# Writing out the first column group of a QKV projection piece by piece, in another order and with part of the work on GpSimd

## The chip, the cores and the metric

The kernel runs on one core of one Trainium2 chip. The metric is the device time of one launch in microseconds (us). Three runs of the kernel before gave 1294.83, 1295.52 and 1296.1; the median is 1295.52 us.

## The reference

2048 tokens with 576 channels, all float32. The input is normalised once, `xn = layernorm(x)`, and two branches of `xn` are added to `x`:

```
def _A_ref(x, wqkv, wo):              # 32 heads of 18, window 8, dilation 2
    qkv = x @ wqkv                    # 576 -> 1728
    ...                               # softmax over 8 dilated earlier positions
    return o @ wo

def _B_ref(x, w1, w2, w3, w4):
    h = gelu(layernorm(x) @ w1)       # 576 -> 576, its quarters shifted by +1, -1, +2, -2 tokens
    x1 = x + shifted(h) @ w2
    return x1 + gelu(layernorm(x1) @ w3) @ w4     # 576 -> 4608 -> 576

return x + _A_ref(xn, wqkv, wo) + _B_ref(xn, w1, w2, w3, w4)
```

The change touches only the beginning of `xn @ wqkv`: the first 288 of its 1728 output columns for the first 512 tokens.

## The kernel before, in words

**Split products.** Every float32 operand of a matrix product is split into a high part (the value rounded to TensorE's fp32r type) and a low part (value minus high part). A product is the sum of high*high, high*low and low*high. The inner dimension of 576 is cut into four slices of 128 and a tail of 64. In the tail, partitions 0 to 63 hold the high part of the tokens and 64 to 127 their low part, against weight rows that are loaded twice. So there are ten slots of weights (0 to 3 high, 4 the tail's high, 5 to 8 low, 9 the tail's low) and nine of tokens, and a tile of 128 tokens by 288 columns takes the 14 matmuls in `PAIRS`: four high*high, four high*low, four low*high and two of the tail.

**Stages.** The kernel goes through the QKV projection (with the transposed second layer norm), the mixer's first product with its shifts, its second product, then the MLP in 36 chunks of the hidden dimension with the attention woven in on VectorE, and the output projection. Instructions of each engine stay in the order in which the code issues them (`manual_schedule`); what an instruction must wait for is a semaphore of the engine or DMA that makes its data or frees its buffer.

**The stage of the change.** Tokens come in tiles of 128 (`load_x`, three buffers `xin`). For tiles 0 to 3, `stats` (L83 to L90) takes mean and variance on VectorE (two `bn_stats`, one `bn_aggr`, one add) and the inverse square root on GpSimd (L89, a `pow` on 128x1); `norm_x` (L96) writes the normalised tile to `Y`. `prep_x` calls `transposes` (L98 to L117): four TensorE transposes (L104) and one of the tail (L107) into PSUM, ScalarE copies the high parts to `xt` (L109 main, L112 tail), VectorE subtracts to get the low parts (L113 main, L116 tail). The weights come in column groups (`COLS`: 288, 288, 288, 432, 432 columns): `load_cg` loads one, `split_cg` has ScalarE write the high part (L167) and VectorE the low part (L168). `q_cg` (L276) makes the 14 matmuls of one tile and one group, ordered high*high, high*low, low*high, tail; ScalarE copies the result to `stg` (L279) and SP stores it (`spill`, L264). A `mid` function can be put before the last three matmuls of a `q_cg`; tiles 2 and 3 are transposed there.

**Order before.** VectorE: stats of tiles 0 and 1, norms 0 and 1, low parts of weight slices 0 to 3, token low parts of tile 0, weight slice 4, stats 2, token low parts 1, norm 2, stats 3, token low parts 2, norm 3, token low parts 3, then the low parts of column group 1. TensorE: 24 warming transposes, the transposes of tiles 0 and 1, then the 14 matmuls of tile after tile with the transposes of tiles 2 and 3 inside. After tile 3, the other column groups follow (`for cg in range(1, 5)`) with tokens that are all there.

Of the kernel before, what the change touches and what calls it, by code (L numbers as in the profile page):

```python
# [8 lines left out]
F32 = mybir.dt.float32  # L9
F32R = mybir.dt.float32r  # L10
AF = mybir.ActivationFunctionType
ALU = mybir.AluOpType
# [28 lines left out]
def dram_ap(t, offset, dims):  # L41
    return bass.AP(tensor=t.tensor, offset=t.offset + offset, ap=[list(d) for d in dims])
# [3 lines left out]
def fused_block(ctx, tc, x, wqkv, wo, w1, w2, w3, w4, out):  # L46
    nc = tc.nc
    pe, act, dve, pool, sp = nc.tensor, nc.scalar, nc.vector, nc.gpsimd, nc.sync
# [6 lines left out]
    psa = ctx.enter_context(tc.tile_pool(name="psa", bufs=2, space=PSUM))  # L55
    psb = ctx.enter_context(tc.tile_pool(name="psb", bufs=3, space=PSUM))
    dram = ctx.enter_context(tc.tile_pool(name="dram", bufs=1, space=DRAM))

    Y = base.tile([128, NT, D], F32, name="Y")
    ident = base.tile([128, 128], F32, name="ident")  # L60
# [13 lines left out]
    def tail_half(t):  # L74
        if t % 2 == 0:
            ztail[t // 2] = qpool.tile([128, 128], F32, name="ztail", bufs=2)
        return ztail[t // 2][:, t % 2 * 64:t % 2 * 64 + 64]

    def pair_tail(src, xts, t):
        return (src, [(xts, (t % 4 - 1) * 128), (xts, (t % 4) * 128)]) if t % 2 else None  # L80

    def stats(src, kind, t):
        st = BN[:, bncnt[0] % 4]  # L83
        bncnt[0] += 1
        for h in range(2):
            dve.bn_stats(out=st[:, h, :], in_=src[:, h * HF:(h + 1) * HF])
        dve.bn_aggr(out=MV[kind][:, t, :], in_=st)
        dve.tensor_scalar(RS[kind][:, t, 0:1], MV[kind][:, t, 1:2], 1e-5, None, op0=ALU.add)
        pool.tensor_tensor(RS[kind][:, t, 1:2], RS[kind][:, t, 0:1], mhalf, op=ALU.pow)  # L89
        if kind == 2:  # L90
            neg = MV[kind][:, t, 0:1]
            dve.tensor_scalar(neg, neg, -1.0, None, op0=ALU.mult)
            pool.tensor_tensor(RS[kind][:, t, 0:1], neg, RS[kind][:, t, 1:2], op=ALU.mult)

    def norm(dst, src, kind, t):
        dve.tensor_scalar(dst, src, MV[kind][:, t, 0:1], RS[kind][:, t, 1:2],  # L96
                          op0=ALU.subtract, op1=ALU.mult)

    def transposes(src, tail, xt, col):
        ps = psb.tile([128, 2, 512], F32, name="ps", tag="b")  # L100
        p0 = ps[:, 0, :].rearrange("p (k c) -> p k c", k=4)
        p1 = ps[:, 1, :128]
        for k in range(4):
            pe.transpose(p0[:, k, :], src[:, k * 128:(k + 1) * 128], ident)  # L104
        rows = tail[0].shape[1] if tail else 0
        if tail:
            pe.transpose(p1[:rows], tail[0], ident)  # L107
        c = slice(col, col + 128)
        act.copy(xt[:, 0:4, c], p0)  # L109
        for i in range(rows // 64):  # L110
            xtt, ct = tail[1][i]
            act.copy(xtt[0:64, 4, ct:ct + 128], p1[64 * i:64 * i + 64])  # L112
        dve.tensor_tensor(xt[:, 5:9, c], p0, xt[:, 0:4, c].bitcast(F32), op=ALU.subtract)  # L113
        for i in range(rows // 64):
            xtt, ct = tail[1][i]
            dve.tensor_tensor(xtt[64:128, 4, ct:ct + 128], p1[64 * i:64 * i + 64],  # L116
                              xtt[0:64, 4, ct:ct + 128].bitcast(F32), op=ALU.subtract)  # L117
# [48 lines left out]
    def split_w(dst_hi, dst_lo, raw):  # L166
        act.copy(dst_hi, raw)  # L167
        dve.tensor_tensor(dst_lo, raw, dst_hi.bitcast(F32), op=ALU.subtract)  # L168

    def dup_tail(dst, w, col, n):  # L170
        ncols = w.shape[1]
        for a in range(2):
            sp.dma_start(dst[64 * a:64 * a + 64, :],
                         dram_ap(w, 512 * ncols + col, [[ncols, 64], [1, n]]))

    def main_rows(dst, w, col, n, k0=0, k1=4):
        sp.dma_start(dst, w[k0 * 128:k1 * 128, col:col + n].rearrange("(k p) c -> p k c", p=128))
# [19 lines left out]
    qpool = qp.__enter__()  # L197
    WQ = qpool.tile([128, 10, 3 * D], F32R, name="WQ")
    xtile = {}
    xring = {}  # L200
    CG = 432
    COLS = [(0, 288), (288, 288), (576, 288), (864, 432), (1296, 432)]

    def load_x(t):
        xtile[t] = qpool.tile([128, D], F32, name="xin", bufs=3)
        sp.dma_start(xtile[t], xf[t * 128:(t + 1) * 128, :])

    def norm_x(t):
        norm(Y[:, t, :], xtile[t], 0, t)
        if t >= 4:  # L210
            dve.tensor_copy(tail_half(t), Y[:, t, 512:])

    def ring_block(key):
        if key not in xring:
            xring[key] = ring.tile([128, 9, 512], F32R, name="xt", tag="xt")
        return xring[key]

    def prep_x(t):
        xt = ring_block(("q", t // 4))
        if t < 4:  # L220
            tail = (Y[:, t, 512:], [(xt, t * 128)])
        else:
            tail = pair_tail(ztail[t // 2], xt, t)
        transposes(Y[:, t, :], tail, xt, (t % 4) * 128)

    qraw = {}

    def load_cg(cg, pieces):
        c, n = COLS[cg]
        r = qraw[cg] = qpool.tile([128, 5, n], F32, name="raw", bufs=2)  # L230
        if pieces:
            main_rows(r[:, 0:2, :], wqkv, c, n, 0, 2)
            main_rows(r[:, 2:4, :], wqkv, c, n, 2, 4)
        else:
            main_rows(r[:, 0:4, :], wqkv, c, n)
        dup_tail(r[:, 4, :], wqkv, c, n)

    def split_cg(cg, k0, k1):
        c, n = COLS[cg]
        split_w(WQ[:, k0:k1, c:c + n], WQ[:, 5 + k0:5 + k1, c:c + n], qraw[cg][:, k0:k1, :])  # L240
# [17 lines left out]
    def lhs(t):  # L258
        xt = xring[("q", t // 4)]
        c = (t % 4) * 128  # L260
        return lambda s: xt[:, s, c:c + 128]

    def spill(stg, t, c0, n):
        sp.dma_start(qkvd[c0 // GC:(c0 + n) // GC, HALO + t * 128:HALO + (t + 1) * 128, :]  # L264
                     .rearrange("s p d -> p s d"),
                     stg.rearrange("p (s d) -> p s d", d=GC))

    def q_cg(t, cg, mid=None):
        ps = psb.tile([128, 2, 512], F32, name="ps", tag="b")
        xs = lhs(t)  # L270
        c, n = COLS[cg]
        pairs = sorted(PAIRS, key=lambda p: (p[0] >= 4, p[1] >= 4))
        for i, (a, b) in enumerate(pairs):
            if mid and i == 11:
                mid()
            pe.matmul(ps[:, 0, :n], xs(a), WQ[:, b, c:c + n],  # L276
                      start=i == 0, stop=i == len(pairs) - 1)
        stg = qpool.tile([128, 2 * CG], F32, name="stg", bufs=4)
        act.copy(stg[:, :n], ps[:, 0, :n])  # L279
        spill(stg[:, :n], t, c, n)  # L280
# [10 lines left out]
    def x_stage(t):  # L291
        norm_x(t)
        prep_x(t)
        stats(Y[:, t, :], 1, t)
# [23 lines left out]
    warm = psa.tile([128, 512], F32, name="p1", tag="a")  # L318
    for i in range(24):
        pe.transpose(warm[:, :128], ident, ident)  # L320
    stats(xtile[0], 0, 0)
    stats(xtile[1], 0, 1)
    norm_x(0)
    norm_x(1)
    split_cg(0, 0, 1)
    split_cg(0, 1, 2)
    split_cg(0, 2, 3)
    split_cg(0, 3, 4)
    prep_x(0)
    split_cg(0, 4, 5)  # L330
    stats(xtile[2], 0, 2)
    prep_x(1)
    q_cg(0, 0)
    norm_x(2)
    load_x(4)
    load_cg(2, False)
    stats(xtile[3], 0, 3)
    q_cg(1, 0, lambda: prep_x(2))
    norm_x(3)
    q_cg(2, 0, lambda: prep_x(3))  # L340
    split_cg(1, 0, 3)
    split_cg(1, 3, 5)
    load_cg(3, False)
    q_cg(3, 0)
    sp.dma_start(dram_ap(qkvd[8:9, 0:1, :], 0, [[(HALO + S) * GC, 16], [1, HALO * GC]]), zpad)
    for cg in range(1, 5):
        for t in range(4):
# [123 lines left out]
    for b in range(NB):  # L471
        for i, m in enumerate((0, 1, 2, 4, 3) if b < 3 else (4, 0, 1, 2, 3)):
# [12 lines left out]
            k = {(0, 4): 0, (1, 1): 1, (1, 4): 2, (2, 1): 3, (2, 4): 4}.get((b, i))  # L485
# [46 lines left out]
    for t in range(NT):  # L532
        ps = psb.tile([128, 2, 512], F32, name="ps", tag="b")

        def xs(a, t=t):
            if a == 4:
                return T4[:, 2 + t * 128:2 + (t + 1) * 128]
            p, g = divmod(a, 5)
            c = 2 + t * 128 - SHIFT[g]
            return H[p][g][:, c:c + 128]  # L540
# [12 lines left out]
        if t in (9, 10, 13, 14):  # L553
            k = {9: 4, 10: 6, 13: 8, 14: 10}[t]
# [280 lines left out]
    for t in range(NT):  # L835
        b, s = divmod(t, 4)
# [7 lines left out]
        if t < NT - 1:  # L844
            ps = psb.tile([128, 2, 512], F32, name="ps", tag="b")
# [3 lines left out]
        else:  # L849
            for h in range(2):  # L850
                ph = psa.tile([128, 512], F32, name="p1", tag="a")
                for i, (a, w) in enumerate(PAIRS):
                    pe.matmul(ph[:, :HF], oT(a), Wo[:, w, h * HF:(h + 1) * HF],  # L853
                              start=i == 0, stop=i == len(PAIRS) - 1)
# [30 lines left out]
```

## Time and profile before

| what | value |
|---|---|
| median of three runs | 1295.52 us (1294.83 to 1296.1) |
| the profiled execution's own time | 1294.73 us |
| its span, first to last instruction | 1292.9 us |
| TensorE (PE) busy | 1285.0 us, 99% |
| weight load (PEld) busy | 1184.8 us, 92% |
| VectorE (DVE) busy | 935.6 us, 72% |
| ScalarE (ACT) busy | 362.0 us, 28% |
| GpSimd (POOL) busy | 38.1 us, 3% |
| granted TensorE clock | 0.9 or more of full speed in all slices (1.000 as the core's mean) |

A line of the timeline reads: start in us from the span's start, duration in us, engine, line of the kernel, operation, output and inputs by the program's names, shapes, how many such instructions were merged into the row, and in brackets how long the engine was idle before and what released it. PE is the matmul and PEld the loading of its stationary operand, which runs beside the matmul before. Matmuls are pipelined, so their durations overlap; the starts of weight loads show the pace. In the view by windows, "(x)" is the number of instructions that lie in the stretch.

### The profile page before, as it was taken

The page shows a single profiled execution, that of the slowest core. Times are in us where ns is not written, and L with a number is a line of the kernel's source. Part 1 is how long each engine was busy: PE and PEld are TensorE (multiplying, and loading weights), DVE is VectorE, ACT ScalarE, POOL GpSimd, SP SyncE. Part 2 cuts the span into 40 slices and gives each one's busy share as a digit, 9 for nine tenths or more (in the row PEclk, how much of TensorE's full clock was granted, in tenths as well). Part 3 has the DMA queues.
Part 4 walks back from the last instruction along what each step waited for, and adds up shares of the span by engine and source line. Part 5 has one row for each costly group of instructions (what it writes and reads, how often), then busy time and mean ns, then how long its engine had stood idle before and what let it go on. Part 6 is the DMA issues. An engine that isn't in the chain of part 4 may idle for free.

```text
span 1292.9 us, 18505 instructions
## 1 busy us (share of the span) xinstructions
PE 1285.0 (99%) x7678; PEld 1184.8 (92%) x7678; DVE 935.6 (72%) x1336; ACT 362.0 (28%) x601; POOL 38.1 (3%) x108
## 2 busy tenths in 40 slices
PE   8999999999999999999999999999999999999998
PEld 8999998899899999989999999999998999999998
DVE  6455534689576778888878888878888878855741
ACT  3332126524412232232222132232232231213310
POOL 2011100021000000000000000000000000000000
PEclk9999999999999999999999999999999999999999
DMA  7646884346702030221221221221232111156842
GB/s 204 154 122 137 172 174 143 92 108 155 229 29 73 29 101 20 82 75 46 82 73 48 82 72 42 89 73 29 75 99 71 31 49 44 58 120 158 208 145 83
DMA packets 157828, 125.20 MB, mean 97 GB/s; under 512 B 72608, under 2 KB 129824, under 8 KB 157744
## 3 DMA queue, kind: packets, MB, share of 16 engines
q1 hardware_dynamic: 157744, 124.02, 34.9%
q8 instruction: 60, 0.98, 0.3%
q14 instruction: 24, 0.20, 0.0%
HBM read 83.56 MB, written 39.39 MB: 95 GB/s over the span
## 4 chain that ended last, share of the span: by engine, by line
PE 94%; DMA 2%; DVE 2%; ACT 1%; SPq 0%; issue 0%; ACTq 0%
PE ps L696 35%; PE p L676 34%; PE ps L182 17%; PE ps L431 4%; PE ps L276 3%; DMA xd<-st 1%; PE ps L446 1%; PE ps L104 1%; DMA xt<-xd 0%; DMA raw<-in_A_wqkv_dram 0%; DMA x1n<-xd 0%; DVE st L129 0%; SPq L137 0%; PE p L853 0%; ACT rz L523 0%
## 5 line engine op out<-in xcount | busy, mean ns | idle before, releaser
L696 PE MATMUL ps<-W,hi 128*128 128x288 f32 x2304 | 398.7, 294 | 0.5 <-DVE Y L699 0.4
L696 PEld LDWEIGHTS ps<-W,hi 128*128 128x128 f32 x2304 | 339.5, 188 | 7.2 <-DVE Y L699 1.0
L680 ACT ACTIVATE hi<-p 128x512 fp32r<-128x512 f32 x144 | 86.2, 598 | 578.4 <-PE p L676 578.4
L696 PE MATMUL ps<-W,lo 128*128 128x288 f32 x1152 | 245.3, 294 | 0.0
L676 PE MATMUL p<-x1n,W 128*128 128x512 f32 x1008 | 234.6, 389 | 0.0
L676 PE MATMUL p<-xt,W 128*128 128x512 f32 x1008 | 234.4, 389 | 0.0
L676 PEld LDWEIGHTS p<-xt,W 128*128 128x128 f32 x1008 | 187.3, 188 | 36.9
L676 PEld LDWEIGHTS p<-x1n,W 128*128 128x128 f32 x1008 | 187.3, 188 | 36.8
L699 DVE TENSOR_TENSOR Y<-ps,Y 128x576 f32<-128x576 f32 x288 | 212.0, 748 | 11.0 <-PE ps L696 10.7
L682 DVE TENSOR_TENSOR lo<-g,hi 128x512 fp32r<-128x512 f32 x144 | 99.5, 691 | 159.5 <-ACT g L681 159.4
L696 PEld LDWEIGHTS ps<-W,lo 128*128 128x128 f32 x1152 | 185.3, 187 | 0.0
L182 PE MATMUL ps<-WQ,xt 128*128 128x432 f32 x672 | 134.4, 359 | 0.0
L182 PEld LDWEIGHTS ps<-WQ,xt 128*128 128x128 f32 x672 | 125.5, 188 | 5.4
L628 DVE TENSOR_TENSOR prod<-q,k 128x1152 f32<-128x1152 f32 x64 | 86.4, 1349 | 0.0
L631 DVE TENSOR_REDUCE L<-prod 128x64 f32<-128x1152 f32 x64 | 86.1, 1346 | 0.0
L681 ACT ACTIVATE g<-p 128x512 f32<-128x512 f32 x144 | 85.3, 592 | 0.0
L612 DVE TENSOR_TENSOR o<-o,prod 128x1152 f32<-128x1152 f32 x56 | 75.5, 1349 | 0.0
L608 DVE TENSOR_TENSOR prod<-v,L 128x1152 f32<-128x1152 f32 x56 | 75.5, 1348 | 0.0
L167 ACT CAST W<-rawf 128x640 fp32r<-128x640 f32 x72 | 50.3, 700 | 70.5 <-PE ps L696 69.2
L168 DVE TENSOR_TENSOR W<-rawf,W 128x640 fp32r<-128x640 f32 x72 | 56.2, 783 | 0.0
L182 PE MATMUL ps<-W,h 128*128 128x288 f32 x384 | 53.5, 295 | 0.0
L182 PEld LDWEIGHTS ps<-W,h 128*128 128x128 f32 x384 | 51.9, 188 | 0.1
(108 smaller groups left out, 888.7 us busy)
## 6 DMA issues: line engine op xcount, KB each, us to landing
xd<-st SPq DMA_DIRECT2D x48, 320.0 KB, 6.0
qkvd<-stg SPq DMA_DIRECT2D x24, 432.0 KB, 3.6
rawf<-in_B_w_dram SPq DMA_DIRECT2D x36, 288.0 KB, 3.2
rawf<-in_B_w_dram SPq DMA_DIRECT2D x36, 256.0 KB, 3.0
xt<-xd SPq DMA_DIRECT2D x8, 768.0 KB, 5.1
xin<-in_A_x_dram SPq DMA_DIRECT2D x16, 288.0 KB, 3.8
q<-qkvd SPq DMA_DIRECT2D x8, 576.0 KB, 4.0
k<-qkvd SPq DMA_DIRECT2D x8, 576.0 KB, 5.0
```

The costliest lines, as they stand in the source:

```text
L168: dve.tensor_tensor(dst_lo, raw, dst_hi.bitcast(F32), op=ALU.subtract)
L182: pe.matmul(ps[:, h, :n], xs(a), ws(b, h), start=i == 0, stop=i == len(PAIRS) - 1)
L608: dve.tensor_tensor(dst, vv, Lf[:, :, w:w + 1].to_broadcast([128, TPP * GH, HD]), op=ALU.mult)
L612: dve.tensor_tensor(o, o, dst, op=ALU.add)
L628: dve.tensor_tensor(prod.rearrange("p (j h) d -> p j (h d)", h=GH), q, k[:, r0:r0 + TPP, :], op=ALU.mult)
L631: dve.tensor_reduce(Lf[:, :, w], prod, axis=AX.X, op=ALU.add)
L676: pe.matmul(ps, W3[f][:, w, :], x1n[b][:, a, :], start=n == 0, stop=n == len(PAIRS) - 1)
L680: act.activation(by_token(hi), in_order(ps), AF.Gelu_apprx_tanh)
L681: act.activation(by_token(g32), in_order(ps), AF.Gelu_apprx_tanh)
L682: dve.tensor_tensor(lo, g32, hi.bitcast(F32), op=ALU.subtract)
L696: pe.matmul(ps[:, k, :HF], h[:, col], w[:, p, k * HF:(k + 1) * HF], start=n == 0, stop=n == len(seq) - 1)
L699: dve.tensor_tensor(yv, ps[:, :, :HF], yv, op=ALU.add)
```

## The change

Only the part for tiles 0 to 3 and column group 0 is written anew. `stats` is cut in two functions (`bn_halves` and `moments`) with the same instructions. In place of `split_cg(0, ...)`, `prep_x(0..3)` and `q_cg(0..3, 0)`, single pieces are issued:

- the low parts of weight slices 0, 1, 2 and 4 are GpSimd's (`w_lo(pool, k)`), that of slice 3 stays VectorE's;
- the products of tiles 0 and 1 accumulate in two PSUM buffers of the pool `psa` at the same time, in parts (`HH` high*high, `HL` high*low, `LH` low*high, `TL` tail), and their tails come after the transposes of tile 2;
- VectorE's norm 0 goes ahead of the last steps of stats 1, and the token low parts of tile 0 ahead of everything after norm 1;
- ScalarE's order is weight slices 0 and 1, tokens of tile 0, weight slices 2 and 3, the tail of tile 0, weight slice 4, tiles 1 and 2, and then the two results of tiles 0 and 1;
- on SP, the load of tile 4 and that of column group 2 are issued ahead of the first three stores, not after the first of them.

The number of instructions is the same on ScalarE; on VectorE it is less by four and on GpSimd more by four.

```
+    def w_lo(eng, k):
+        eng.tensor_tensor(WQ[:, 5 + k, c0:c0 + n0], qraw[0][:, k, :],
+                          WQ[:, k, c0:c0 + n0].bitcast(F32), op=ALU.subtract)
...
+    def x_lo(t):
+        p0, p1, c = main_tail(t)
+        dve.tensor_tensor(xt0[:, 5:9, c], p0, xt0[:, 0:4, c].bitcast(F32), op=ALU.subtract)
+        dve.tensor_tensor(xt0[64:128, 4, c], p1, xt0[0:64, 4, c].bitcast(F32), op=ALU.subtract)
...
     stats(xtile[0], 0, 0)
-    stats(xtile[1], 0, 1)
+    st1 = bn_halves(xtile[1])
     norm_x(0)
+    x_turned(0)
+    w_hi(0)
+    w_hi(1)
+    moments(st1, 0, 1)
+    w_lo(pool, 0)
+    w_lo(pool, 1)
+    x_hi(0)
+    w_hi(2)
+    w_hi(3)
+    x_tail_hi(0)
+    w_hi(4)
     norm_x(1)
-    split_cg(0, 0, 1)
-    split_cg(0, 1, 2)
-    split_cg(0, 2, 3)
-    split_cg(0, 3, 4)
-    prep_x(0)
-    split_cg(0, 4, 5)
+    q_part(0, HH, True)
+    x_turned(1)
+    x_lo(0)
+    q_part(0, LH)
+    w_lo(pool, 2)
+    x_hi(1)
+    x_tail_hi(1)
     stats(xtile[2], 0, 2)
-    prep_x(1)
-    q_cg(0, 0)
+    w_lo(dve, 3)
+    w_lo(pool, 4)
+    q_part(1, HH, True)
+    q_part(0, HL)
+    x_lo(1)
+    q_part(1, LH)
+    q_part(1, HL)
     norm_x(2)
     load_x(4)
     load_cg(2, False)
+    x_turned(2)
     stats(xtile[3], 0, 3)
-    q_cg(1, 0, lambda: prep_x(2))
+    x_hi(2)
+    x_tail_hi(2)
+    q_part(0, TL)
+    q_out(0)
+    q_part(1, TL)
+    q_out(1)
+    q_part(2, HH, True)
+    q_part(2, HL)
+    x_lo(2)
+    q_part(2, LH)
     norm_x(3)
-    q_cg(2, 0, lambda: prep_x(3))
+    x_turned(3)
+    q_part(2, TL)
+    x_hi(3)
+    x_tail_hi(3)
+    q_out(2)
+    x_lo(3)
     split_cg(1, 0, 3)
     split_cg(1, 3, 5)
     load_cg(3, False)
-    q_cg(3, 0)
+    for pairs in (HH, HL, LH, TL):
+        q_part(3, pairs, pairs is HH)
+    q_out(3)
```

`x_turned`, `x_hi` and `x_tail_hi` hold the instructions of `transposes`, `w_hi` and `w_lo` those of `split_w`, `q_part` and `q_out` those of `q_cg`.

More of the change, by code (lines that the diff above doesn't have):

```diff
@@ L82, in stats, with bn_halves @@
     def stats(src, kind, t):
+        moments(bn_halves(src), kind, t)
+    def bn_halves(src):
         st = BN[:, bncnt[0] % 4]
@@ L86, in stats, with moments @@
             dve.bn_stats(out=st[:, h, :], in_=src[:, h * HF:(h + 1) * HF])
+        return st
+    def moments(st, kind, t):
         dve.bn_aggr(out=MV[kind][:, t, :], in_=st)
@@ L320, in fused_block, with w_hi, main_tail @@
         pe.transpose(warm[:, :128], ident, ident)
+    c0, n0 = COLS[0]
+    xt0 = ring_block(("q", 0))
+    tps, qps = {}, {}
+    def w_hi(k):
+        act.copy(WQ[:, k, c0:c0 + n0], qraw[0][:, k, :])
+    def w_lo(eng, k):
+        eng.tensor_tensor(WQ[:, 5 + k, c0:c0 + n0], qraw[0][:, k, :],
+                          WQ[:, k, c0:c0 + n0].bitcast(F32), op=ALU.subtract)
+    def main_tail(t):
+        c = slice(t * 128, t * 128 + 128)
+        return (tps[t][:, 0, :].rearrange("p (k c) -> p k c", k=4), tps[t][:64, 1, :128], c)
@@ new lines, in x_turned, with x_hi, x_tail_hi @@
+    def x_turned(t):
+        tps[t] = psb.tile([128, 2, 512], F32, name="ps", tag="b")
+        p0, p1, c = main_tail(t)
+        for k in range(4):
+            pe.transpose(p0[:, k, :], Y[:, t, k * 128:(k + 1) * 128], ident)
+        pe.transpose(p1, Y[:, t, 512:], ident)
+    def x_hi(t):
+        p0, p1, c = main_tail(t)
+        act.copy(xt0[:, 0:4, c], p0)
+    def x_tail_hi(t):
+        p0, p1, c = main_tail(t)
+        act.copy(xt0[0:64, 4, c], p1)
+    def x_lo(t):
+        p0, p1, c = main_tail(t)
+        dve.tensor_tensor(xt0[:, 5:9, c], p0, xt0[:, 0:4, c].bitcast(F32), op=ALU.subtract)
+        dve.tensor_tensor(xt0[64:128, 4, c], p1, xt0[0:64, 4, c].bitcast(F32), op=ALU.subtract)
@@ new lines, in fused_block, with q_part, q_out @@
+    HH = [(k, k) for k in range(4)]
+    HL = [(k, k + 5) for k in range(4)]
+    LH = [(k + 5, k) for k in range(4)]
+    TL = [(4, 4), (4, 9)]
+    def q_part(t, pairs, first=False):
+        if first:
+            qps[t] = psa.tile([128, 512], F32, name="p1", tag="a")
+        xs = lhs(t)
+        for i, (a, b) in enumerate(pairs):
+            pe.matmul(qps[t][:, :n0], xs(a), WQ[:, b, c0:c0 + n0], start=first and i == 0,
+                      stop=pairs is TL and i == len(TL) - 1)
+    def q_out(t):
+        stg = qpool.tile([128, 2 * CG], F32, name="stg", bufs=4)
+        act.copy(stg[:, :n0], qps[t][:, :n0])
+        spill(stg[:, :n0], t, c0, n0)
```

## The prediction

> **What bounds the kernel now.** First the page's busy shares, then a table by windows, then the timeline of the first 21 us engine by engine (the stage of the change), and the chain of waits between its rows.
>
> ```profile
> PE 1285.0 (99%) x7678; PEld 1184.8 (92%) x7678; DVE 935.6 (72%) x1336; ACT 362.0 (28%) x601; POOL 38.1 (3%) x108
> ```
> ```profile
> 0.00:20.45 20.45, 16.26 (x101) 14.32 (x102) 13.14 (x34) 8.38 (x19) 4.72 (x22) 1.00 0.69 202
> ```
>
> TensorE is busy 1285.0 us, and the profiled execution took 1294.73 us with a span of 1292.9 us, so 7.9 us of the span are idle. In the window up to 20.45 us 16.26 us are busy: 4.19 us of the idle time lie there, in what this change rewrites. After it the kernel is bound by matmuls, so a microsecond won or lost here reaches the end nearly whole; but 4.19 us, 0.3%, is all that there is to win, and the part of it before the first tile has arrived is out of reach.
>
> Inside the stage VectorE sets the pace. Its timeline:
>
> ```profile
> 6.05 0.21 DVE L87 BATCH_NORM_AGGREGATE mv<-bn 128x2 f32<-128x12 f32 x1
> 6.30 0.15 DVE L88 TENSOR_SCALAR rs<-mv 128x1 f32<-128x1 f32 x1
> 6.37 0.57 DVE L96 TENSOR_SCALAR Y<-xin,mv,rs 128x576 f32<-128x576 f32 x1
> 7.38 0.58 DVE L96 TENSOR_SCALAR Y<-xin,mv,rs 128x576 f32<-128x576 f32 x1 [0.44 <-POOL rs L89]
> 7.88 1.56 DVE L168 TENSOR_TENSOR WQ<-raw,WQ 128x288 fp32r<-128x288 f32 x4
> 9.35 0.69 DVE L113 TENSOR_TENSOR xt<-ps,xt 128x512 fp32r<-128x512 f32 x1
> 10.07 0.28 DVE L116 TENSOR_TENSOR xt<-ps,xt 64x128 fp32r<-64x128 f32 x1
> 10.39 0.46 DVE L168 TENSOR_TENSOR WQ<-raw,WQ 128x288 fp32r<-128x288 f32 x1
> 10.77 0.81 DVE L86 BATCH_NORM_STATS2 bn<-xin 128x6 f32<-128x288 f32 x2
> ...
> 11.94 0.69 DVE L113 TENSOR_TENSOR xt<-ps,xt 128x512 fp32r<-128x512 f32 x1
> 12.66 0.28 DVE L116 TENSOR_TENSOR xt<-ps,xt 64x128 fp32r<-64x128 f32 x1
> 12.98 0.58 DVE L96 TENSOR_SCALAR Y<-xin,mv,rs 128x576 f32<-128x576 f32 x1
> ...
> 15.25 0.69 DVE L113 TENSOR_TENSOR xt<-ps,xt 128x512 fp32r<-128x512 f32 x1 [0.54 <-ACT xt L112]
> 15.97 0.28 DVE L116 TENSOR_TENSOR xt<-ps,xt 64x128 fp32r<-64x128 f32 x1
> 16.29 0.58 DVE L96 TENSOR_SCALAR Y<-xin,mv,rs 128x576 f32<-128x576 f32 x1
> ```
>
> Up to norm 2 at 12.98 it hardly pauses. From there on it is a chain through three engines: norm, transposes, ScalarE's copies, VectorE's token low parts, next norm, 3.31 us from norm 2 (12.98) to norm 3 (16.29). The weight loads and ScalarE show the other links:
>
> ```profile
> 13.67 0.42 PEld L104 LDWEIGHTS ps<-ident,Y 128*128 128x128 f32 x4 [0.56 <-issue]
> ...
> 16.98 0.42 PEld L104 LDWEIGHTS ps<-ident,Y 128*128 128x128 f32 x4 [0.38 <-issue]
> ...
> 18.43 2.82 PEld L276 LDWEIGHTS ps<-WQ,xt 128*128 128x128 f32 x21 [0.51 <-ACT xt L109]
> ```
> ```profile
> 7.09 0.76 ACT L167 CAST WQ<-raw 128x288 fp32r<-128x288 f32 x2 [0.46 <-DMA raw<-in_A_wqkv_dram]
> 7.80 0.59 ACT L109 CAST xt<-ps 128x512 fp32r<-128x512 f32 x1
> 8.28 0.26 ACT L112 CAST xt<-ps 64x128 fp32r<-64x128 f32 x1
> ...
> 14.47 0.58 ACT L109 CAST xt<-ps 128x512 fp32r<-128x512 f32 x1 [2.74 <-PE ps L107]
> 14.96 0.26 ACT L112 CAST xt<-ps 64x128 fp32r<-64x128 f32 x1
> 15.11 0.40 ACT L279 COPY stg<-ps 128x288 f32<-128x288 f32 x1
> ```
>
> From norm start to transposes 0.69 us (12.98 to 13.67), from these to the main copy 0.80 (14.47), to the token low parts 0.78 more (15.25), to the next norm 1.04 (16.29). Tile 3's products start at 18.43, and 2.82 us for 21 weight loads is 0.134 us each: from there the engine runs without pause. So the change is worth what it moves the transposes of tile 3, at 16.98 before.
>
> **The change part by part.** I follow the new order with these durations.
>
> *Norm 0 earlier.* It needs the bn_stats ahead of it (over by 6.05) and GpSimd's pow (over at 6.01, row below): 6.05 in place of 6.37, 0.32 us won. By tile 0's own rows (6.37 to 7.80, 1.43) ScalarE's main copy starts at 7.48. Statistics 1 end after it: aggregate at 6.55 (a norm holds VectorE 0.50, 7.38 to 7.88), add 0.25 later, pow from 7.03 (0.23 after the add) to 7.58, norm 1 from 7.61 to 8.19, 0.23 later than before. That is harmless: the transposes of tile 1 now stand behind four matmuls which wait for weight slice 3, until about 8.9.
>
> *ScalarE's order.* After the main copy (0.48, 7.80 to 8.28) come weight slices 2 and 3 (0.71, 7.09 to 7.80), then the tail: 8.67 to 8.93. The built program lets the token low parts wait for the tail copy, as the row at 15.25 does. So they start at 8.96 and not at 9.35; VectorE idles before them from 8.1.
>
> *VectorE with four subtractions less.* Four of 0.39 (1.56 for four) go to GpSimd; two waits come in their place (0.66 before norm 1, 0.9 before the token low parts). From 8.96: token low parts 1.04 (11.94 to 12.98), statistics 2 1.17 (10.77 to 11.94), slice 3 0.38 (10.39 to 10.77), token low parts of tile 1 1.04. **Norm 2 at 12.59 against 12.98**: 0.39 us won of 1.56 taken away.
>
> *GpSimd's subtractions.* The trace before has none of 128x288. Its nearest rows:
>
> ```profile
> L93 POOL TENSOR_TENSOR rs<-mv,rs 128x1 f32<-128x1 f32 x16 | 3.1, 195 | 1.3
> ...
> masks.py:199 POOL TENSOR_SCALAR_AFFINE_SELECT ident<-ident 128x128 f32<-128x128 f32 x1 | 0.3, 292 | 0.1
> ```
> ```profile
> 5.45 0.56 POOL L89 TENSOR_TENSOR rs<-rs,mhalf 128x1 f32<-128x1 f32 x1 [2.41 <-DVE rs L88]
> 6.53 0.82 POOL L89 TENSOR_TENSOR rs<-rs,mhalf 128x1 f32<-128x1 f32 x1 [0.53 <-DVE rs L88]
> 12.09 0.55 POOL L89 TENSOR_TENSOR rs<-rs,mhalf 128x1 f32<-128x1 f32 x1 [4.74 <-DVE rs L88]
> ...
> 264.80 1.18 POOL L89 TENSOR_TENSOR rs<-rs,mhalf 128x1 f32<-128x1 f32 x1 [1.19 <-DVE mv L92]
> ```
> ```profile
> 264.74 1.49 DVE L168 TENSOR_TENSOR W<-rawf,W 128x640 fp32r<-128x640 f32 x2
> ```
>
> An instruction with one input takes 0.292 us for 128 columns, so 0.66 for 288; doubled for the second input it is 1.31. The low bound is VectorE's own 0.39, the high one the pow's 0.55 as a fixed cost on top of 1.31, 1.86. I take 0.9, nearer to 0.66 because only the read doubles and the fixed part (0.195 for one column) counts once. Pow rows also show a wait between the two engines: 0.55 beside the token low parts (12.09), but 0.82 beside a norm and 1.18 beside L168, with the end 0.41 after the norm's (7.35 against 6.94).
>
> The Trainium skill, "GPSIMD Engine Reference", section "Performance versus the Vector engine", speaks against the move: a two-input add of 2048 columns is given as 4497 ns, about twice VectorE's. An estimate from it is 0.63 us for 288 columns; the sum would stand at the early end below. No row here shows it.
>
> After norm 1 (8.19) slices 0 to 2 take until 10.89. The pow of tile 2 comes 1.32 after statistics 2 start (10.77 to 12.09), so at 11.32, and is stretched by VectorE's slice 3 to 11.63 + 0.41 = 12.04. Slice 4 then lasts until 12.95, and norm 2 wants to start at 12.59. Either they run side by side, or norm 2 waits until 12.95. I keep both.
>
> For the same case the skill's "SBUF — State Buffer", section "Who interferes with whom", has a rule: the shared port pair is locked for a whole instruction and the later one blocks. The stretched pows agree (0.82 and 1.18 against 0.55); it gives the 12.95, the late end below.
>
> *TensorE behind norm 2.* In front of the transposes of tile 2 now stand eight matmuls of tile 1, which start when its token low parts are there (11.55 + 0.69 and 0.06 of latency, 12.30) and take 8 x 0.134: 13.37. The norm alone would allow 12.59 + 0.69 = 13.28 or 12.95 + 0.69 = 13.64. So 13.37 or 13.64, against 13.67. Main copy 14.17 or 14.44.
>
> *A new wait.* The pool `psa` has two buffers. Tile 2's products take that of tile 0, so their first matmul waits until `q_out(0)` has read it, and that copy stands on ScalarE behind both copies of tile 2: 0.64 after the main copy (14.47 to 15.11), 0.40 long, 0.05 of latency. Tile 2's first matmul: 15.26 or 15.53, against 15.11 before (0.06 after the main copy). Behind it are queued its twelve matmuls of the main slices (1.61) and the transposes of tile 3: 16.87 or 17.14. Norm 3 follows 0.78 + 1.04 = 1.82 after the main copy (15.99 or 16.26) and would have allowed 16.68 or 16.95. **Transposes of tile 3 at 16.87 or 17.14, against 16.98.** From there to tile 3's products and group 1 the links are as before.
>
> *SP.* The load of tile 4 waits only for norm 1 and leaves earlier, behind tile 3's on the same queue. That of column group 2 waits now for GpSimd's slice 4 too (12.95, the end of VectorE's old slice 4 having been 10.85); its data is wanted after group 1 starts, 14 x 0.134 after 18.43, so 7 us cover it. Three stores leave later, and their staging buffers (four) are wanted again in group 1. I cost all this at nothing; if a buffer were late, ScalarE's copies and then PSUM would be, by as much as the transfer.
>
> *Sum.* 0.11 us earlier or 0.16 later than 1294.73: no change within what these rows can tell, 1294.7. The median of the runs shown lies 0.8 above that execution, so against it **1295.5 us**.
>
> **Rivals.**
>
> 1. *A small gain.* Norm 2 isn't held up, and the wait for `q_out(0)` is hidden because the matmuls go faster than 0.134. Then norm 3 decides, 0.3 to 0.4 us earlier: 1295.1. For it: 0.39 us are there at norm 2. Against: the eight and twelve matmuls stand in front of the transposes. More than 2.6 us would need most of the 4.19 idle us, with the chain of 3.31 us a tile unchanged.
> 2. *GpSimd is too slow (slower).* Place: the pow of tile 2 stands behind slices 0 to 2 on GpSimd. It ends at 8.19 + 3w + 0.55; norm 2 is late when that passes 12.59, from w = 1.28 us. At the high bound, 1.86, the pow ends at 14.32; norm 2 goes first, slice 4 then runs from 14.93 to 16.79, tile 0's tail waits for it, `q_out(0)` for that (17.6), and tile 2 for that: transposes of tile 3 at 19.3, 2.3 us late; with slice 4 ahead of norm 2, about 3.4. About 2.8: 1297.5 by the execution, 1298.3 by the median. For it: the pow's 0.55 for one column and the stretched pows. Against: 0.292 for 128 columns.
> 3. *The edit does not do what it says:* the program's order shows the moves, so only their effect is open.
>
> **How the numbers follow.** A measurement of this kernel can tell about 0.2%, 2.6 us, from no change. Forecast (0.3 earlier to 0.6 later): 0.70. Rival 1: 0.14, of it 0.02 beyond 2.6 us. Rival 2: 0.16, of it 0.09 beyond 2.6 us, since the threshold is 1.28 and only the upper third of the bounds reaches so far. Faster 0.02, same 0.89, slower 0.09. The range takes in rival 1 with the runs' own spread of 0.7 below the median, and rival 2 up to w of about 1.6: 1294.0 to 1297.6.
>
> **What would show it.** Right: norm 0 near 6.05, token low parts of tile 0 near 8.96 after a pause that ends on ScalarE, norm 2 between 12.6 and 12.95, tile 2's first matmul released by the copy to `stg`, transposes of tile 3 near 17. GpSimd's rows near 0.9 us decide rival 2: over 1.3 I am wrong on the slow side. Group 1's first matmul well before 19.5 us would make me wrong on the fast side.

## The result, and the profile after

| | before | after |
|---|---|---|
| median of twelve runs | 1294.87 us (1294.02 to 1296.1) | 1297.66 us (1296.94 to 1298.83) |
| ratio, 95% interval | | **1.0023 [1.0015, 1.0031]** |
| profiled execution's own time, span | 1294.73, 1292.9 us | 1298.83, 1297.1 us |

The changed kernel is 2.79 us slower by the medians. No change was forecast, and 1297.66 lies 0.06 us above the range that was given. The first lines of the profile after (TensorE's busy time is nearly the same, so the loss is idle time):

```profile
span 1297.1 us, 18505 instructions
PE 1286.0 (99%) x7678; PEld 1184.7 (91%) x7678; DVE 934.6 (72%) x1332; ACT 362.0 (28%) x601; POOL 41.5 (3%) x112
```

A table by windows tells which stage holds it. The stretch is followed by its length, then by TensorE's busy time in it. After:

```profile
0.00:20.45 20.45, 16.40 (x100) 14.41 (x101) 12.11 (x30) 8.29 (x19) 7.88 (x26) 1.00 0.72 202
195.00:260.00 65.00, 62.24 (x277) 50.57 (x276) 35.61 (x48) 37.12 (x61) 0.83 (x18) 1.00 0.37 109
260.00:1290.00 1030.00, 1029.01 (x6328) 948.76 (x6327) 796.31 (x1023) 268.36 (x438) 14.26 (x40) 1.00 0.29 84
```

The same stretches of before, without the first, which the prediction shows with 16.26 us busy:

```profile
195.00:260.00 65.00, 65.00 (x306) 54.55 (x305) 39.03 (x54) 39.63 (x65) 0.75 (x18) 1.00 0.43 122
260.00:1290.00 1030.00, 1029.19 (x6326) 948.55 (x6325) 794.39 (x1021) 265.71 (x433) 14.20 (x40) 1.00 0.29 84
```

The stage that was rewritten is as busy as before, and so are the last 1030 us. The idle time is between 195 and 260 us, in the mixer's first product, **some 180 us behind the last line that the change touches**.

**The rewritten stage did what was forecast.** Its clock starts with the landing of the first tile of tokens, which differs from one execution to the next: the first `bn_stats` of before starts at

```profile
4.04 0.82 DVE L86 BATCH_NORM_STATS2 bn<-xin 128x6 f32<-128x288 f32 x2 [4.04 <-DMA xin<-in_A_x_dram]
```

and that of after at 4.23, which is 0.19 us later. VectorE's timeline of after:

```profile
4.23 0.82 DVE L89 BATCH_NORM_STATS2 bn<-xin 128x6 f32<-128x288 f32 x2 [4.23 <-DMA xin<-in_A_x_dram]
...
6.24 0.58 DVE L102 TENSOR_SCALAR Y<-xin,mv,rs 128x576 f32<-128x576 f32 x1
...
7.79 1.04 DVE L102 TENSOR_SCALAR Y<-xin,mv,rs 128x576 f32<-128x576 f32 x1 [0.67 <-POOL rs L95]
9.12 0.69 DVE L362 TENSOR_TENSOR xt<-ps,xt 128x512 fp32r<-128x512 f32 x1 [0.28 <-ACT xt L358]
...
11.31 0.45 DVE L338 TENSOR_TENSOR WQ<-raw,WQ 128x288 fp32r<-128x288 f32 x1
...
12.71 0.58 DVE L102 TENSOR_SCALAR Y<-xin,mv,rs 128x576 f32<-128x576 f32 x1
```

GpSimd's, with the three subtractions of slices 0 to 2 in one row and slice 4 in the last:

```profile
7.72 2.52 POOL L338 TENSOR_TENSOR WQ<-raw,WQ 128x288 fp32r<-128x288 f32 x3
11.47 0.69 POOL L95 TENSOR_TENSOR rs<-rs,mhalf 128x1 f32<-128x1 f32 x1 [1.22 <-DVE rs L94]
12.13 0.80 POOL L338 TENSOR_TENSOR WQ<-raw,WQ 128x288 fp32r<-128x288 f32 x1
```

And TensorE's weight loads (L349 transposes, L375 products):

```profile
13.45 0.49 PEld L349 LDWEIGHTS ps<-ident,Y 128*128 128x128 f32 x4
...
15.42 1.63 PEld L375 LDWEIGHTS p<-WQ,xt 128*128 128x128 f32 x12 [0.83 <-ACT stg L380]
16.99 0.49 PEld L349 LDWEIGHTS ps<-ident,Y 128*128 128x128 f32 x4
...
18.50 1.89 PEld L375 LDWEIGHTS p<-WQ,xt 128*128 128x128 f32 x14 [0.64 <-ACT xt L354]
```

Tile 3's products start 18.50 - 4.23 = 14.27 us after the first `bn_stats`; before it was 18.43 - 4.04 = 14.39. The stage is 0.12 us shorter than before, and in this execution a later first load takes that back. The difference is small but it repeats: of the kernels below, e1 has the stage of before and gives 14.38, e2, e4 and e5 have the stage of after and give 14.26, 14.25 and 14.25 (e3 14.35, where ScalarE's first weight slice came 2.72 us after the first `bn_stats`, in the others 1.53 to 2.13).

**Where the time went.** At 195 us the QKV projection ends and the mixer's first product begins. ScalarE before (L286 the projection's last result, L436 and L437 the first activations):

```profile
195.32 0.88 ACT L286 COPY stg<-ps 128x864 f32<-128x864 f32 x1 [4.63 <-PE ps L182]
196.22 1.28 ACT L436 ACT_TABLE_LOAD   x1
198.46 0.60 ACT L436 ACTIVATE h<-ps 128x512 fp32r<-128x512 f32 x1 [0.96 <-PE ps L431]
198.96 0.59 ACT L437 ACTIVATE g<-ps 128x512 f32<-128x512 f32 x1
```

ScalarE after:

```profile
195.39 0.89 ACT L292 COPY stg<-ps 128x864 f32<-128x864 f32 x1 [4.63 <-PE ps L188]
198.58 1.28 ACT L532 ACT_TABLE_LOAD   x1 [2.30 <-PE ps L527]
199.87 0.60 ACT L532 ACTIVATE h<-ps 128x512 fp32r<-128x512 f32 x1
203.87 0.60 ACT L533 ACTIVATE g<-ps 128x512 f32<-128x512 f32 x1 [3.40 <-DMA qkvd<-stg]
```

Two things are new: the table load waits 2.30 us for TensorE, and the first write of `g` waits 3.40 us for a store of `stg`, a buffer that it has nothing to do with by name. The chain that ended last passes through this store (start, duration, what):

```profile
196.33 7.46 DMA qkvd<-stg
...
203.82 0.04 issue
203.87 0.61 ACT g L533
```

It is the projection's last store, and SP issued it behind two loads (`xt<-xd`; by the DMA issues of the trace they carry 768 and 512 KB, and the store 432 KB):

```profile
195.34 0.89 SPq L148 DMA_DIRECT2D xt<-xd  x2
196.33 0.42 SPq L270 DMA_DIRECT2D qkvd<-stg  x1
```

The store itself is no slower than it was: in before it stands behind the same two loads and lands 7.8 us after its issue. There nothing waits for it.

While ScalarE waits, the high parts of the next block of tokens (L160) and with them VectorE's low parts (L161) come late, SP issues the loads of the block after that at 215.61 where it was 212.59 in before, and TensorE in the end waits for low parts. Its first long wait is at 227.70. All its waits of over half a microsecond behind 30 us but one lie here (us in total, times, longest):

```profile
PEld ps L527 <- DVE xt L161: 1.5, 1, 1.5
PEld ps L542 <- DVE xt L161: 1.4, 1, 1.4
PEld ps L792 <- DVE Y L795: 1.2, 1, 1.2
PEld ps L542 <- ACT g L533: 1.0, 1, 1.0
PEld ps L542 <- ACT xt L160: 0.6, 1, 0.6
```

Before had one such row at this place:

```profile
PEld ps L446 <- DVE xt L155: 0.4, 1, 0.4
```

In the chain of after the mixer's second product starts at 258.20:

```profile
258.20 52.00 PE ps L188 x392
```

In the chain of before it starts at 254.41:

```profile
254.41 37.14 PE ps L182 x280
```

That is 3.79 us of the 4.2 us between the spans. The profiled execution of after is the slowest of its twelve, so the medians lie closer.

### The profile page after: what moved, and what is told of

It reads as the page before. It is cut to its first block, busy times and chain, and to the rows that moved or that the text cites. A ratio compares the mean times of both kernels' runs of the same rounds, so it can differ in the third digit from the quotient of the medians.

```text
span 1297.1 us, 18505 instructions
## 1 busy us (share of the span) xinstructions
PE 1286.0 (99%) x7678; PEld 1184.7 (91%) x7678; DVE 934.6 (72%) x1332; ACT 362.0 (28%) x601; POOL 41.5 (3%) x112
## 4 chain that ended last, share of the span: by engine, by line
PE 93%; DMA 3%; DVE 2%; ACT 1%; SPq 1%; issue 0%; POOL 0%; DVEq 0%; ACTq 0%; POOLq 0%
PE ps L792 35%; PE p L772 34%; PE ps L188 18%; PE ps L282 3%; PE ps L527 1%; DMA xt<-xd 1%; DMA qkvd<-stg 1%; DMA xd<-st 0%; PE p L375 0%; PE ps L110 0%; DMA x1n<-xd 0%; SPq L548 0%; SPq L547 0%; ACT xt L160 0%; PE p L949 0%
## 5 line engine op out<-in xcount | busy, mean ns | idle before, releaser
L527 PE MATMUL ps<-xt,W 128*128 128x512 f32 x224 | 51.9, 390 | 1.1 <-DVE xt L161 1.1
```

The source lines that it names most:

```text
L527: pe.matmul(ps, W1[:, w, m * 128:(m + 1) * 128], xt[:, a, :], start=i == 0, stop=i == len(PAIRS) - 1)
```

## The experiments

**What the built programs say.** The staging buffers `stg` are freed when the projection ends, and the mixer's buffers are laid over the same memory. In the built program of before the last store reads its staging buffer at bytes 143840 to 147296 of a partition and the store before it at 140384 to 143840. In after the two have changed places. The mixer's `g32`, the buffer of the first `g`, lies at 141248 to 143296 in both. So in before its first write has to wait for the last store but one, which landed long ago, and in after for the last one, which has just been issued. A second difference: GpSimd now also writes weights (`WQ`), and in the built program the mixer's first activation has a wait for GpSimd that it had not before; its wait for TensorE stands ahead of the table load.

**Theory M** (memory): the loss is the wait of `g32` for the store. **Rival T** (table load): the loss is the 1.28 us load that starts later. **Rival S** (stage): the rewritten stage itself, by GpSimd's port or the new order, costs the time. Four kernels cross the first two suspects, before and after. Each time stands beside the median of the kernel before that was measured together with it.

**e1: before, with the memory moved.** An unused tile moves the mixer's buffers so that `g32` lies on the last store's buffer, in the kernel before.

```
     mupool = mup.__enter__()
+    mupool.tile([128, 648], F32, name="pad")
```

> The kernel before, with an unused tile of 2592 bytes a partition ahead of g32 in the mixer's pool, so that the first g32 lies on the staging buffer of the projection's last store and no longer on that of the store before it; the first column group is untouched. Theory M (the loss comes from g32 waiting for the last store): 2 to 3 us slower than before, about 1297.3, the first write of g32 waits until about 203.8. Rival S (the loss comes from the rewritten first stage): same as before within 0.5 us. Rival T (from the table load's wait): same as before within 0.5 us.

Measured: 1297.17 us against 1294.17, ratio 1.0025 [1.0015, 1.0035]. The table load is where it was; ScalarE's timeline of this kernel:

```profile
195.73 1.28 ACT L437 ACT_TABLE_LOAD   x1
...
203.39 0.60 ACT L438 ACTIVATE g<-ps 128x512 f32<-128x512 f32 x1 [4.81 <-DMA qkvd<-stg]
```

An unused tile, with nothing of the change, gives the whole loss.

**e2: after, with the same tile**, which there moves `g32` off the last store's buffer. The same edit.

> The changed kernel with the same unused tile, which here takes g32 off the last store's buffer; ScalarE's table load still waits for the mixer's first product. Theory M: the loss goes, 1294.9 to 1295.4. Rival T: half of the loss stays, since the table load's 1.28 us still stand behind the matmuls, 1296.2. Rival S: as the changed kernel, 1297.7.

Measured: 1294.32 us against 1294.17, ratio 1.0 [0.9991, 1.0009]. ScalarE's timeline:

```profile
197.99 1.28 ACT L533 ACT_TABLE_LOAD   x1 [2.30 <-PE ps L528]
...
199.78 0.59 ACT L534 ACTIVATE g<-ps 128x512 f32<-128x512 f32 x1
```

The late table load is still there and the loss is gone. The time is below the 1294.9 to 1295.4 that was expected, as before itself is lower here (1294.17).

**e3: after, with the table load put back.** ScalarE reads one column of GpSimd's weights early, so that the wait for GpSimd is done with by the time of the mixer.

```
     load_w1(1)
+    seen = qpool.tile([128, 1], F32, name="seen")
+    act.copy(seen, WQ[:, 9, 0:1].bitcast(F32))
     for t in range(4, NT):
```

> The changed kernel with one ScalarE copy of one column of GpSimd's last low part, long before the mixer, so that the mixer's first activation needs no wait on GpSimd and its table load none on TensorE; g32 still lies on the last store's buffer. Theory M: as the changed kernel, 1297.4 to 1297.7, the table load back near 196.3. Rival T: 1.3 us faster than the changed kernel, 1296.3. Rival S: 1297.7.

Measured: 1298.03 us against 1294.17, ratio 1.0028 [1.0017, 1.0039]. The table load is early again, the wait for the store is not:

```profile
195.76 1.28 ACT L534 ACT_TABLE_LOAD   x1
...
204.16 0.60 ACT L535 ACTIVATE g<-ps 128x512 f32<-128x512 f32 x1 [5.55 <-DMA qkvd<-stg]
```

**e4: after, with both edits.**

> The changed kernel with the unused tile and the early ScalarE copy. Theory M and rival T: as before within 0.4 us, 1294.9 (the first stage is level by the trace, 18.50 against 18.43 for tile 3's first product). Rival S: 1297.7.

Measured: 1294.18 us against 1294.17, ratio 1.0 [0.9991, 1.0009]. With e2 this says that the late table load costs nothing that can be measured (1294.32 and 1294.18), and that the rewritten stage costs nothing either: T and S fall. As to S, tile 3's products start at 17.85, 14.25 us after the first `bn_stats` (3.60).

**e5: after, with the last store ahead of the loads.** Theory M has two parts: where `g32` lies, and how late the store lands. This one leaves the memory as it is and makes the store earlier.

```
+        spill(stg, t, 2 * h * CG, 2 * CG)
         if t == NT - 1 and h == 1:
             get(("z", 1), ring_block(("z", 1)))
-        spill(stg, t, 2 * h * CG, 2 * CG)
```

> The changed kernel with the projection's last store issued ahead of the two loads of the second token block and not behind them; g32 still lies on its buffer. If the wait was long because the store stood behind 768 KB of loads on the queue, the first write of g32 starts near 200.5 in place of 203.9 and most of the loss goes: 1295.0. If the store is slow by itself, the wait stays and with it the loss: 1297.5.

Measured: 1294.58 us against 1294.67, ratio 1.0 [0.9991, 1.0009]. SP's queue:

```profile
196.20 0.36 SPq L270 DMA_DIRECT2D qkvd<-stg  x1
196.65 1.77 SPq L148 DMA_DIRECT2D xt<-xd  x2
```

ScalarE's timeline, in which the row of `g` has no wait:

```profile
200.26 0.59 ACT L533 ACTIVATE g<-ps 128x512 f32<-128x512 f32 x1
```

The store is issued at almost the same moment as in after (196.20 against 196.33), but no load is ahead of it (the two carry 1280 KB together, not the 768 of the expectation). It lands 3.9 us after its issue, near 200.1, and `g` waits for nothing. So the loads ahead of the store are the other half of the loss. The margin is thin: `g` starts at 200.26 because the table load is late here too. With an early table load, as in before (`g` at 198.96), about 1.1 us of waiting would be left by this estimate; no run has that pair.

How long the mixer's first product takes in each profiled execution, from the start of the projection's last copy on ScalarE to the first product behind it in the chain:

| kernel | `g32` on the last store's buffer | that store behind the loads | table load waits | us | median against before |
|---|---|---|---|---|---|
| before | no | yes | no | 254.41 - 195.32 = 59.09 | |
| after | yes | yes | yes | 258.20 - 195.39 = 62.81 | +2.79 |
| e1 | yes | yes | no | 257.03 - 194.83 = 62.20 | +3.00 |
| e2 | no | yes | yes | 253.76 - 194.80 = 58.96 | +0.15 |
| e3 | yes | yes | no | 256.98 - 194.86 = 62.12 | +3.86 |
| e4 | no | yes | no | 253.69 - 194.75 = 58.94 | +0.01 |
| e5 | yes | no | yes | 254.33 - 195.29 = 59.04 | -0.09 |

Only where both of the first two columns say yes is the time lost.

**What the stage itself can give.** The other five start from e4, so that the loss at the mixer is out of the way. They ask whether the prediction's links inside the stage hold, and whether its 4.19 idle us can be reached. Times of the whole kernel cannot tell 0.2 us here; starts in the traces can. Two yardsticks: tile 3's first product counted from the first `bn_stats`, and the same counted from the token low parts of tile 0, which leaves out how early ScalarE's weight slices came. The second repeats too: 9.37 or 9.38 us in after and in e2 to e5, all with the same stage.

**e6: e4, with tile 2's products in a PSUM buffer of another pool**, which takes away the wait for `q_out(0)`.

```
-            qps[t] = psa.tile([128, 512], F32, name="p1", tag="a")
+            qps[t] = (psb.tile([128, 2, 512], F32, name="ps", tag="b")[:, 0, :] if t == 2 else
+                      psa.tile([128, 512], F32, name="p1", tag="a"))
```

> The kernel of e4 with tile 2's products in a PSUM buffer of the other pool, so that their first matmul no longer waits for the copy of tile 0's result. If that wait is what gives back the gain at norm 2, tile 2's first matmul starts 0.4 us earlier against its main copy (0.64 after its start, not 1.09) and tile 3's first product about 0.15 us earlier; the time 1294.0. If norm 3 decides there, tile 3's product moves by less than 0.05 us.

Measured: 1294.14 us against 1294.67, ratio 0.9998 [0.9989, 1.0007]. The wait of tile 2's first product has changed hands, by the weight loads:

```profile
14.74 1.62 PEld L376 LDWEIGHTS ps<-WQ,xt 128*128 128x128 f32 x12 [0.38 <-ACT xt L354]
```

Tile 2's first product now idles 0.38 us for the token copy, not 0.83 for `stg`. From the token low parts of tile 0 to tile 3's products it is 18.05 - 8.89 = 9.16 us, in e4 17.85 - 8.48 = 9.37: the new wait was worth 0.21. In this execution ScalarE's first weight slice came at 6.79 (5.30 in e4) and the token low parts of tile 0 0.41 us later than in e4, which took back more than that: from the first `bn_stats` it is 14.45.

**e7: e4, with all five low parts on VectorE again.**

```
-    w_lo(pool, 0)
+    w_lo(dve, 0)
...
-    w_lo(pool, 1)
+    w_lo(dve, 1)
...
-    w_lo(pool, 2)
+    w_lo(dve, 2)
...
-    w_lo(pool, 4)
+    w_lo(dve, 4)
```

> The kernel of e4 with all five low parts of the weights on VectorE, in the same places. What GpSimd takes over is then seen by itself: four subtractions of 0.39 us, less VectorE's pauses before norm 1 and the token low parts of tile 0: norm 2 and tile 3's first product 0.8 to 1.5 us later against the start of the first statistics than in e4; the time 1295.0 to 1295.7. If GpSimd's share is worth nothing: 1294.2.

Measured: 1295.17 us against 1294.67, ratio 1.0003 [0.9995, 1.0012]. The weight loads of tile 3's products:

```profile
18.83 1.89 PEld L375 LDWEIGHTS p<-WQ,xt 128*128 128x128 f32 x14 [0.64 <-ACT xt L354]
```

Tile 3's products start 18.83 - 3.81 = 15.02 us after the first `bn_stats`, 0.77 later than in e4, just under the 0.8 to 1.5 expected; counted from the token low parts of tile 0 it is 0.77 as well. So GpSimd's share is worth 0.77 us of the new order, which without it would be slower than before (14.39).

**e8: e6, with the tail of tile 0 copied ahead of weight slices 2 and 3.**

```
     x_hi(0)
+    x_tail_hi(0)
     w_hi(2)
     w_hi(3)
-    x_tail_hi(0)
     w_hi(4)
```

> The kernel of e6 with ScalarE's tail copy of tile 0 ahead of weight slices 2 and 3, so that VectorE's token low parts of tile 0 wait for norm 1 alone: they start 0.2 to 0.3 us earlier, norm 2 and tile 3's first product with them; the time 1293.8. If GpSimd holds norm 1 longer, nothing moves.

Measured: 1294.05 us against 1294.67, ratio 0.9996 [0.9987, 1.0005]. The same row here:

```profile
17.87 1.89 PEld L376 LDWEIGHTS p<-WQ,xt 128*128 128x128 f32 x14 [0.64 <-ACT xt L354]
```

The token low parts start at 8.70, 4.52 us after the first `bn_stats` (4.18), against 4.88 in e4 (0.36 us earlier, where 0.2 to 0.3 was expected), and tile 3's products after 17.87 - 4.18 = 13.69: 0.56 better than e4, of which 0.21 is e6's edit, and 0.70 better than before. The stage can be shortened, but a whole-kernel ratio of 0.9996 cannot be told from 1.

**e9: e8, with GpSimd's first subtraction after norm 1.** In after, norm 1 took 1.04 us beside a GpSimd subtraction, and 0.58 elsewhere. Here GpSimd begins behind ScalarE's slice 2.

```
-    w_lo(pool, 0)
-    w_lo(pool, 1)
     x_hi(0)
     x_tail_hi(0)
     w_hi(2)
+    w_lo(pool, 2)
+    w_lo(pool, 0)
+    w_lo(pool, 1)
     w_hi(3)
     w_hi(4)
...
-    w_lo(pool, 2)
```

> The kernel of e8 with GpSimd's order slice 2, 0, 1 (all after ScalarE's high part of slice 2), so that none of its subtractions is ready when norm 1 starts. If the 1.04 us of norm 1 were a wait for GpSimd's running subtraction, norm 1 takes 0.58 again and the token low parts of tile 0 start 0.3 us earlier against the first statistics (4.2 us after them, 4.52 in e8); GpSimd's slice 4 then holds norm 2 up to 0.5 us, so tile 3's first product gains 0 to 0.3. The time 1293.8 to 1294.1. If norm 1 was long for another reason, nothing moves.

Measured: 1294.62 us against 1294.46, ratio 0.9998 [0.9989, 1.0007]. VectorE's timeline:

```profile
7.70 0.58 DVE L102 TENSOR_SCALAR Y<-xin,mv,rs 128x576 f32<-128x576 f32 x1 [0.67 <-POOL rs L95]
...
10.56 0.81 DVE L338 TENSOR_TENSOR WQ<-raw,WQ 128x288 fp32r<-128x288 f32 x1
```

GpSimd's three subtractions:

```profile
8.74 2.32 POOL L338 TENSOR_TENSOR WQ<-raw,WQ 128x288 fp32r<-128x288 f32 x3 [1.08 <-ACT WQ L335]
```

Norm 1 is back at 0.58, but GpSimd now runs until 11.06 and VectorE's own subtraction beside it takes 0.81 in place of 0.45. Tile 3's products start 17.89 - 4.14 = 13.75 us after the first `bn_stats`, no earlier than in e8 (13.69), although the token low parts of tile 0 start at 4.22 as expected. The stretch has moved to another instruction.

**e10: e9, with slice 4 after the last pow and the tails of tiles 0 and 1 behind tile 2's other products.**

```
-    w_lo(pool, 4)
...
-    q_part(0, TL)
-    q_out(0)
-    q_part(1, TL)
-    q_out(1)
+    w_lo(pool, 4)
     q_part(2, HH, True)
     q_part(2, HL)
     x_lo(2)
     q_part(2, LH)
     norm_x(3)
+    q_part(0, TL)
+    q_out(0)
+    q_part(1, TL)
+    q_out(1)
```

> The kernel of e9 with GpSimd's slice 4 behind the pow of tile 3, and the tail products and result copies of tiles 0 and 1 behind tile 2's other products. Norm 2 takes 0.58 and starts right behind the token low parts of tile 1; tile 3's first product 13.2 to 13.5 us after the first statistics (14.39 before, 13.69 in e8); the time about 1 us below the kernel before, 0.9992. If the transposes of tile 3 are late through TensorE's four tail products, no more than e9.

Measured: 1294.43 us against 1294.46, ratio 1.0002 [0.9993, 1.0011]. Tile 3's products start 18.31 - 3.62 = 14.69 us after the first `bn_stats`, where 13.2 to 13.5 was expected. The expectation's second branch is what came, as the weight loads of the tails (L376) and of tile 3's transposes (L349) show:

```profile
16.26 0.59 PEld L376 LDWEIGHTS p<-WQ,xt 128*128 128x128 f32 x4
16.79 0.49 PEld L349 LDWEIGHTS ps<-ident,Y 128*128 128x128 f32 x4
```

The four tail products stand right ahead of the transposes of tile 3, which norm 3 (15.86, and 0.69 from a norm to its transposes) would have allowed at 16.55. Tile 3's products start 18.31 - 8.47 = 9.84 us after the token low parts; in e9 it was 17.89 - 8.36 = 9.53. The rest of the miss is in the token low parts themselves, which start 4.85 us after the first `bn_stats` (4.22 in e9); the first four transposes took 0.87 us in this execution (0.43 in e9), and why is not shown.

## Why the prediction was wrong

**The stage, point by point.** After's starts less the 0.19 us by which its first tile came later:

| step | forecast | measured, less 0.19 |
|---|---|---|
| norm 0 | 6.05 | 6.05 |
| norm 1 | 7.61, lasts 0.58 | 7.60, lasts 1.04 |
| token low parts of tile 0 | 8.96, after a wait for ScalarE | 8.93, after a wait for ScalarE |
| GpSimd's slices 0 to 2 | 8.19 to 10.89, after norm 1 | 7.53 to 10.05, from before norm 1 |
| GpSimd's subtraction | 0.9 | 0.80, 1.02, 0.79 and 0.80 |
| norm 2 | 12.59 or 12.95 | 12.52 |
| transposes of tile 2 | 13.37 or 13.64 | 13.26 |
| tile 2's first product, released by `stg` | 15.26 or 15.53 | 15.23 |
| transposes of tile 3 | 16.87 or 17.14 | 16.80 |

The forecast's early branch is what happened, each start of VectorE and TensorE within 0.11 us. Two things were off: the length of norm 1, by 0.46, and its place against GpSimd. The prediction put the subtractions behind norm 1; the first stands right behind the pow of tile 1 on GpSimd, norm 1 waits for the same pow, and the subtraction began 0.07 us ahead of it. Counted from 7.53 the threshold of rival 2 would have been 1.50 us and not 1.28. For the transposes of tile 3 it gave 0.11 us earlier than before; measured from the first `bn_stats` it is (16.99 - 4.23) against (16.98 - 4.04), 0.18 earlier. The new wait for `q_out(0)` was priced rightly as what eats the gain (e6: 0.21).

**Rival 2** had the right sign for another reason. Its threshold was a subtraction of 1.28 us, which none of the four reached, not even the one beside norm 1 (1.02); tile 3's products weren't late. The value taken, 0.9, was 0.10 to 0.11 above the three that weren't stretched. The Trainium skill, "GPSIMD Engine Reference", section "Performance versus the Vector engine", led to an estimate of 0.63 us, which is 0.16 to 0.17 too low for those three.

**The late branch for norm 2** didn't happen: norm 2 started at 12.71, inside GpSimd's row for slice 4 (12.13 to 12.93), and took its usual 0.58. Where a stretch did come is at norm 1, which starts 0.07 us after GpSimd's first subtraction and took 1.04. In after it cost little, because ScalarE's tail copy ended last (the token low parts waited 0.28 for it).

**The step that failed** is that on SP and the stores: "Three stores leave later, and their staging buffers (four) are wanted again in group 1. I cost all this at nothing". Group 1 was indeed not held up. But the buffers have one more user, in another pool: what is laid over them after the pool is closed. The prediction asked whether the four buffers are free in time for group 1, and not which of them holds the last result of the projection; the rewriting makes the last two change places. The closing words of the TensorE step, "From there to tile 3's products and group 1 the links are as before", hold to 0.06 us (from tile 3's transposes to its products 1.45 before, 1.51 after), and the sum was made as if nothing behind group 1 could change. With "after it the kernel is bound by matmuls, so a microsecond won or lost here reaches the end nearly whole" the stage's own 0.1 us was carried to the end, while the loss arose 180 us later in an idle time of 2.76 us (65.00 - 62.24) in a stretch that had none before. What was put at nothing is thus the wait of `g32`'s first write for the last store, 3.40 us in after and 2.79 us of the kernel's time; e1 makes it without the rewriting, and e2 and e5 take it away with the rewriting in place.

The size isn't one number: the store's wait at `g` was 3.40 us in after, 4.81 in e1 and 5.55 in e3 (there from an earlier table load), and the medians lost 2.79, 3.00 and 3.86 us, the last two with intervals that overlap. By the table under e5 the mixer's first product took 3.72, 3.11 and 3.03 us longer than in before. So the loss doesn't follow the length of that wait; how the later waits add up to it isn't worked out here.

**What stays open.** Which of the edits makes the two buffers change places isn't known; the swap is read from the built programs, and that it decides is shown by e1, e2 and e5. GpSimd's share alone doesn't do it: in the built program of e7, which gives that work back to VectorE, the two still stand as in after. The late table load alone, put into the kernel before, wasn't tried; its cost of nothing rests on e2 against e4. No version here is measurably faster than before; the best is e8 with 0.9996 [0.9987, 1.0005].

## What to carry to other kernels

When a change reorders who takes a rotating buffer, follow each buffer past the end of its pool: the next pool lies on the same memory, and its first writer waits for the last reader, here a store. Compare the built programs' placement and waits, and look for a wait on a name that has nothing to do with the instruction (`g` waiting for `stg`). The remedy is cheap: issue the last store of a stage ahead of the next stage's loads (e5, with little margin), or move the next stage's first buffers off it (e2).

## What the runs showed of the hardware

- VectorE and GpSimd hold each other up, and in the first two of these cases it is the later one that is stretched. A 128x576 norm took 1.04 us when it started 0.07 us after a GpSimd subtraction of two operands in SBUF (after), and 0.58 without one (e9). In e6, where the norm started first (7.16), it kept its 0.58, and GpSimd's first subtraction (7.30) took 1.09 in place of 0.80. VectorE's own 128x288 subtraction took 0.81 beside GpSimd's, against 0.45 (e9, after). The Trainium skill, "SBUF — State Buffer", section "Who interferes with whom", gives an exclusive lock of the port pair that the two engines share; these rows agree. Norm 2 in after shows that not every overlap of two rows in the trace is paid for: it started 0.58 us into GpSimd's row of 0.80 and still took 0.58.
- A GpSimd subtraction of 128x288 took 0.79 to 0.80 us where nothing stretched it (after), where VectorE's took 0.39 to 0.46.
- A store of 432 KB landed 7.46 us after its issue behind loads of 768 and 512 KB (after), and 7.5 to 8.3 us after it in the five other kernels with that order (before, e1 to e4). Issued ahead of them it landed after 3.9 us (e5); the median of these stores over the kernel is 3.5 us by after's list of DMA issues.
